# A kept row of squares, one filler fewer and swapped squares in a fused attention and MLP kernel

## The chip, the cores and the metric

The kernel runs on one core of one Trainium2 chip. The metric is the device time of one execution in microseconds (us). Every profile comes from one such execution; its span, from the first to the last instruction, is about 1.8 us shorter than the time of the same execution.

Names used below: PE is TensorE (matmuls), PEld its weight loads, DVE is VectorE, ACT is ScalarE, POOL is GpSimd and SP is SyncE (after the first microseconds both only issue transfers here). L217 is line 217 of the kernel. The changed kernel has one line more, so its lines from 493 on are numbered one higher: L578 before is L579 after.

## The reference, cut to what matters

```python
def _attn_ref(q, k, v, tau):                  # B, N, C = 4, 6080, 256
    qn = q / (np.linalg.norm(q, axis=1, keepdims=True) + 1e-06)
    kn = k / (np.linalg.norm(k, axis=1, keepdims=True) + 1e-06)
    s = kn.transpose(0, 2, 1) @ qn / tau
    ...                                       # softmax over the last axis -> a
    return (v @ a).astype(np.float32)

def _moe_ref(x, w_in, w_out, s, b):           # 24320 rows, 256 -> 2048 -> 256
    r = np.maximum(x @ w_in, 0.0)
    return ((s * (r * r) + b) @ w_out).astype(np.float32)
```

For each of four batches, the norms of q and k along N and the 256x256 product of k and q are needed before any row of that batch can go through the MLP. The kernel folds the softmax matrix into w_in (the result is called wa), so that the MLP runs straight from v.

## The kernel before

PE is the engine to keep fed. It runs 48 groups of up to 512 rows: a first product (h_ps, L578), relu on ACT, squares on DVE or ACT, and a second product (o_ps, L746) in a seven-product form that needs the sums S from DVE (in the first and the last group it is plain: L650, L624). While the groups of one batch run, the next batch's q and k are loaded in 12 chunks, and squares, products and norms are slipped in between by a table of steps.

The squares of one chunk are folded on DVE to one row tile `f` (128 partitions x 512). In batch 0 each row goes into the norm matmuls by itself. In batches 1 to 3 only the first row does: the rows of all later chunks are added into it by accumulating transfers.

```python
def fold(half, arrays, last):
    ...
        if last and (self.b == 0 or c == 0):
            self.rows.append((st["f", half], np_, 1))      # goes into the norm matmuls

def into_first():                                          # L188
    dst, src = self.rows[0][0][:np_], st["f", 1][:np_]
    po(nc.gpsimd.dma_start(out=dst, in_=src, accum_op=ALU.add))
...
ops += [fold(2, slice(0, 2), False), fold(1, slice(0, 2), True)]
return ops + [into_first] if self.b > 0 and c > 0 else ops

def add_norms(self, last=False):
    todo = [(t, np_, j, a, ch) for t, np_, jc in self.rows for j in range(jc)
            for a in range(2) for ch in range(CH)]         # 4 matmuls for each row
    for i, (t, np_, j, a, ch) in enumerate(todo):
        po(nc.tensor.matmul(self.n_ps[:, a, ch : ch + 1], t[:np_, a, j, ts(ch, P)],
                            ones16[:np_, 0:1], ...))       # L217, one column wide
```

At the start nothing else is there for PE. It runs matmuls that nobody reads ("fillers", L417) while DVE and ACT turn batch 0's norms and scores into wa:

```python
fin[1](); fin[2](); fin[3]()
keep_busy(5, w_in16[:, 0, :P], w_in16[:, 0, :NW])   # five 128x512 fillers
fin[4]()                                            # transposes of sm_s (L253)
...
```

In the last group every relu tile has its own square, alternating between DVE and ACT:

```python
if g in plain:
    late = g > 0 and m // 2 % 2 == 1
    square(g, m // 2, m // 2 + 1, nc.scalar if late else nc.vector)
```

Of the kernel before, what the change touches and what calls it, by code (L numbers as in the profile page):

```python
# [16 lines left out]
def kernel(  # L17
# [13 lines left out]
    P = 128  # L31
# [22 lines left out]
    def po(ins):  # L54

        tc.keep_in_program_order(ins)
        return ins
# [25 lines left out]
    w_in16 = wpool.tile([P, CH, Dff], FP16)  # L83
# [4 lines left out]
    def h_tile(name):  # L88
        return ps_h.tile([P, 2, TG], FP32, tag="h_ps", name=name)
# [19 lines left out]
    class Gram:  # L109
# [41 lines left out]
        def norm_ops(self, c):  # L151

            qc, kc = self.tiles[c]
            _, np_, jc = self.chunks[c]
            st = {}

            def squares(a, js):
                def f():
                    if "sq" not in st:
                        st["sq"] = sq_pool.tile([P, 2, JC, C], FP16, tag="sq", name="sq")  # L160
                    if a == 0:
                        po(nc.vector.tensor_mul(
                            st["sq"][:np_, 0, js, :], qc[:np_, js, :], qc[:np_, js, :]))
                    else:
                        po(nc.scalar.activation(  # L165
                            out=st["sq"][:np_, 1, js, :], in_=kc[:np_, js, :], func=AF.Square))
                return f

            def fold(half, arrays, last):
                def f():  # L170
                    src = st["f", 2 * half] if 2 * half < jc else st["sq"]
                    if ("f", half) not in st:
                        if last:
                            t = f3_pool.tile([P, 2, 1, C], FP16, tag="f3", name="f3")
                        else:
                            t = sq_pool.tile([P, 2, half, C], FP16, tag=f"f{half}", name="f")
                        st["f", half] = t
                    po(nc.vector.tensor_add(  # L178
                        st["f", half][:np_, arrays], src[:np_, arrays, :half, :],
                        src[:np_, arrays, half : 2 * half, :]))  # L180
                    if last and (self.b == 0 or c == 0):
                        self.rows.append((st["f", half], np_, 1))
                return f

# [5 lines that stand above are left out]
            def unfolded():  # L190
                self.rows.append((st["sq"], np_, jc))

            ops = []
            for h in range(0, jc, 4):
                js = slice(h, min(h + 4, jc))
                ops += [squares(1, js), squares(0, js)]
            if jc == 2:
                return ops + [unfolded]
            if jc == 8:
                ops += [fold(4, slice(0, 1), False), fold(4, slice(1, 2), False)]  # L200
            ops += [fold(2, slice(0, 2), False), fold(1, slice(0, 2), True)]
            return ops + [into_first] if self.b > 0 and c > 0 else ops

        def add_norms(self, last=False):

# [177 lines left out]
    NW = 512  # L383
# [29 lines left out]
    def keep_busy(n, w, x):  # L413

        idle_ps = h_tile("idle_ps")[:, 0, :]
        for _ in range(n):
            po(nc.tensor.matmul(idle_ps, w, x, start=True, stop=True, skip_group_check=True))  # L417

    for c in range(NCH0):
        ops = g0.norm_ops(c)  # L420
# [12 lines left out]
    fin[1]()  # L433
    fin[2]()
    fin[3]()
    keep_busy(5, w_in16[:, 0, :P], w_in16[:, 0, :NW])
    fin[4]()
    transpose_v(0)
    for f in fin[5:12]:
# [47 lines left out]
    def at_step(s, f):  # L487
        side.setdefault(int(s), []).append(f)


    FIN = (-12, 0, 3, 3, 6, 8, 10, 13)
    first_group = [b * N // TG for b in range(B)]
    for i, f in enumerate(fin[12:]):
        at_step(i // 2 * 4 - 1 + i % 2 if i > 1 else 0, f)
    at_step(14, lambda: po(nc.vector.tensor_scalar_mul(
        out=s_out, in0=s_bc, scalar1=1.0 / (LAM * LAM))))

# [63 lines left out]
    def mm1(g, m):  # L561

        _, nj = group(g)
        n = nj * P
        vT = vT_tiles[g]
        i, fh = divmod(m, 2)
        if fh == 0:
            h_tiles[g, i] = h_tile("h_ps")
        h_ps = h_tiles[g, i][:, fh, :]
        for b, p0, p1 in segments(g):  # L570
            wa = grams[b].wa
            for ci in range(CH):
                if p1 - p0 == P:
                    dst, src = h_ps[:, :n], vT[:, ci, :n]
                else:
                    dst = h_ps[:, :n].rearrange("f (j p) -> f j p", p=P)[:, :, p0:p1]
                    src = vT[:, ci, :n].rearrange("f (j p) -> f j p", p=P)[:, :, p0:p1]
                po(nc.tensor.matmul(dst, wa[:, ci, ts(m, P)], src,  # L578
                                    start=(ci == 0), stop=(ci == CH - 1), skip_group_check=True))  # L579
        if m == FT - 1:  # L580
            del vT_tiles[g]

    def relu(g, i):
        n = group(g)[1] * P
        if i % 2 == 0:
            r_tiles[g, i // 2] = rpool.tile([P, 2, 2, TG], FP16, tag="r16", name="r16")
        r16 = r_tiles[g, i // 2]
        po(nc.scalar.activation(out=r16[:, :, i % 2, :n], in_=h_tiles.pop((g, i))[:, :, :n],  # L588
                                func=AF.Relu))

    def square(g, i0, i1, engine):

        n = group(g)[1] * P
        if i0 == 0:
            g_tiles[g] = gpool.tile([P, 2, NP, TG], FP16, tag="g16", name="g16")
        src = r_tiles[g, i0 // 2][:, :, i0 % 2 : i0 % 2 + i1 - i0, :n]
        dst = g_tiles[g][:, :, i0:i1, :n]
        if engine is nc.scalar:
            po(nc.scalar.activation(out=dst, in_=src, func=AF.Square))  # L599
        else:  # L600
            po(nc.vector.tensor_mul(dst, src, src))  # L601
# [33 lines left out]
    def plain_mm2(g, m):  # L635

        _, nj = group(g)
        if g == NG - 1:
            last_mm2(0, m)
            if m == FT - 1:  # L640
                for i in range(FT):
                    last_mm2(1, i)
            return
        for h in range((nj + 1) // 2):
            js = [j for j in (2 * h, 2 * h + 1) if j < nj]
            if m == 0:
                o_plain[g, h] = ps_o.tile([P, 2, C], FP32, tag="o_ps", name="o_ps")
            o = o_plain[g, h]
            for j in js:
                po(nc.tensor.matmul(  # L650
                    o[:, j % 2, :], g_tiles[g][:, m % 2, m // 2, ts(j, P)],
                    w_out16[:, m, :], start=(m == 0 and j == js[0]),
                    stop=(m == FT - 1 and j == js[-1]), skip_group_check=True))
            if m == FT - 1:
                if h == 0:
                    o_sbs[g] = opool.tile([P, TG // P, C], FP32, tag="o_sb", name="o_sb")
                evacuate(o_sbs[g][:, js[0] : js[-1] + 1, :], o, rowconst, 1)
                if js[-1] == nj - 1:
                    store(g)
# [110 lines left out]
    for s in range(NS + FT):  # L770
        g, m = divmod(s, FT)
        if g < NG:
            mm1(g, m)

        if m == SHIFT and 0 < g and g - 1 not in plain:
            items = seven_items(g - 1)
            work.append((items, 8 if g == NG - 1 else 7))
        if work:
            items, n = work[0]
            for f in items[:n]:  # L780
                f()
            del items[:n]
            if not items:
                work.pop(0)
        for gp in plain:
            for mp in range(FT):
                if s == gp * FT + PLAG[gp] + (mp * 3 // 2 if gp == 0 else mp):
                    plain_mm2(gp, mp)
        if g < NG and m % 2 == 1:
            relu(g, m // 2)  # L790
            if g in plain:
                late = g > 0 and m // 2 % 2 == 1
                square(g, m // 2, m // 2 + 1, nc.scalar if late else nc.vector)
        if g < NG and g not in plain and m in SQUARES:
            square(g, *SQUARES[m])
        if g == NG - 1 and m in LAST:
            LAST[m]()
        elif m == 0 and 0 < g and g - 1 not in plain:
            square(g - 1, 6, 8, nc.vector)
        elif 0 < g and g - 1 not in plain and m in SUMS:  # L800
            sums_of(g - 1, SUMS[m])
        for f in side.pop(s, []):
            f()
# [34 lines left out]
```

## Time and profile before

| | before |
|---|---|
| time, median of 4 runs | 723.98 us (723.40 to 724.46; 723.81 of the three runs known at prediction time) |
| span of the profiled execution | 722.3 us |
| PE busy | 700.6 us (97%) |
| share of PE in the chain that ended last | 89% |
| largest wait of PE after 41 us | 1.4 us, for one accumulating transfer |

The lines that show the waits of PE stand in the prediction. A row of a timeline reads: start, duration, engine, line, operation, out<-in, shape, count, and in brackets the idle time before it with what ended it. Neighbouring instructions of one kind are merged into one row, and the end of a matmul is modelled; so I compare the starts of matmuls, which are not.

### The profile page before, as it was taken

What the parts mean: (1) busy time and instruction counts of PE and PEld (TensorE: products, weight loads), DVE (VectorE), ACT (ScalarE), POOL (GpSimd) and SP (SyncE); (2) the same over time, 40 slices, a digit from 0 to 9 for tenths busy, and PEclk for the clock granted to TensorE, in tenths of its full rate; (3) what the DMA queues carried; (4) which work ended last, traced back from release to release, by engine and by line L of the source; (5) the groups of instructions that cost most, each with busy time, mean ns of one, the idle gap of its engine ahead of it and who ended that gap; (6) DMA issues with size and microseconds to landing.
All of it is one profiled execution on the core that took longest, in us unless ns stands there. A gap on an engine that the chain in (4) does not pass through costs nothing.

```text
span 722.3 us, 17624 instructions
## 1 busy us (share of the span) xinstructions
PE 700.6 (97%) x7486; PEld 505.6 (70%) x7486; DVE 623.0 (86%) x871; ACT 544.8 (75%) x589; POOL 112.5 (16%) x191
## 2 busy tenths in 40 slices
PE   4799999999999999999999999999999999999997
PEld 2556777766677777777677777777668777777777
DVE  4779999988889999998788998998888888888886
ACT  5479877887777777788777777778777777777874
POOL 4522332111101222111010222111000000000000
PEclk9999999999999999999999999999999999999999
DMA  9999998556484979463763777836323333321202
GB/s 235 208 259 141 175 167 146 95 113 126 93 118 98 164 142 143 93 104 78 148 135 76 134 135 127 151 82 95 94 66 78 92 71 74 97 59 47 81 30 75
DMA packets 86447, 83.83 MB, mean 116 GB/s; under 512 B 56240, under 2 KB 61504, under 8 KB 86368
## 3 DMA queue, kind: packets, MB, share of 16 engines
q0 software_dynamic: 26176, 43.74, 37.6%
q1 hardware_dynamic: 59616, 37.64, 21.2%
q8 instruction: 59, 0.97, 0.6%
q10 hardware_dynamic: 576, 1.31, 0.5%
q14 instruction: 20, 0.16, 0.1%
HBM read 78.91 MB, written 24.90 MB: 144 GB/s over the span
## 4 chain that ended last, share of the span: by engine, by line
PE 89%; DMA 6%; issue 2%; DVE 1%; ACT 1%; POOL 1%; POOLq 0%; ACTq 0%
PE h_ps L578 43%; PE o_ps L746 38%; PE s_ps L142 4%; DMA qk<-in_q_dram 2%; PE wa_ps L290 2%; DMA f<-f 1%; DMA w_in<-in_moe_w_in_dram 1%; DMA qk<-in_k_dram 1%; ACT r L588 1%; POOL qk L126 1%; PE o_ps L624 1%; PE o_ps L650 0%; DVE S L672 0%; ACT g L599 0%; DVE o_sb L606 0%
## 5 line engine op out<-in xcount | busy, mean ns | idle before, releaser
L588 ACT ACTIVATE r<-h_ps 128x1024 f16<-128x1024 f32 (+1 forms) x384 | 388.0, 1014 | 144.3 <-PE h_ps L578 142.6
L578 PE MATMUL h_ps<-vT,wa 128*128 128x512 f16 (+7 forms) x1632 | 451.9, 364 | 0.6 <-ACT r L588 0.4
L746 PEld LDWEIGHTS <-S 128*128 128x128 f16 x2944 | 197.9, 98 | 85.2 <-DVE S L672 0.4
L746 PEld LDWEIGHTS <-g 128*128 128x128 f16 x2208 | 155.1, 98 | 74.0
L601 DVE TENSOR_TENSOR g<-r 128x2048 f16<-128x2048 f16 (+2 forms) x150 | 174.7, 1164 | 16.5 <-ACT r L588 16.2
L746 PE MATMUL o_ps<-T,S 128*128 128x128 f16 x2208 | 183.2, 219 | 0.3 <-DVE S L672 0.2
L578 PEld LDWEIGHTS <-wa 128*128 128x128 f16 x1632 | 136.2, 98 | 21.2 <-issue 1.0
L746 PE MATMUL o_ps<-w_out,g 128*128 128x128 f16 x1472 | 134.2, 219 | 0.3 <-DVE u L606 0.3
L606 DVE SCALAR_TENSOR_TENSOR o_sb<-o_ps,s_out,u 128x256 f32<-128x256 f32 x138 | 66.4, 481 | 50.1 <-PE o_ps L746 48.0
L599 ACT ACTIVATE g<-r 128x1024 f16<-128x1024 f16 (+1 forms) x97 | 100.4, 1035 | 0.2
L142 PE MATMUL s_ps<-qk 128*128 128x256 f16 (+1 forms) x384 | 69.4, 280 | 14.5 <-ACT qk L133 6.9
L337 POOL DMA_DIRECT2D v<-in_v_dram x48 | 31.9, 673 | 244.3 <-DMA vT<-v 179.8
L188 POOL DMA_DIRECT2D f<-f x33 | 28.9, 877 | 244.1 <-DVE f L178 186.4
L606 DVE SCALAR_TENSOR_TENSOR u<-o_ps,s_out,rowconst 128x256 f32<-128x256 f32 x138 | 65.9, 478 | 1.1 <-PE o_ps L746 1.1
L746 PE MATMUL o_ps<-w_out,S 128*128 128x128 f16 x736 | 63.5, 219 | 0.0
L746 PE MATMUL o_ps<-N,g 128*128 128x128 f16 x736 | 63.4, 219 | 0.0
L165 ACT ACTIVATE sq<-qk 128x1024 f16<-128x1024 f16 (+3 forms) x49 | 50.5, 1033 | 10.9 <-DMA qk<-in_k_dram 6.3
L674 DVE TENSOR_TENSOR S<-S,g 128x2048 f16<-128x2048 f16 (+1 forms) x47 | 56.4, 1201 | 1.3
L672 DVE TENSOR_TENSOR S<-g 128x2048 f16<-128x2048 f16 (+1 forms) x47 | 56.1, 1193 | 0.0
L678 DVE TENSOR_TENSOR S<-g,S 128x2048 f16<-128x2048 f16 x46 | 55.9, 1215 | 0.0
L676 DVE TENSOR_TENSOR S<-g 128x2048 f16<-128x2048 f16 x46 | 55.8, 1214 | 0.0
L142 PEld LDWEIGHTS <-qk 128*128 128x128 f16 (+1 forms) x384 | 32.5, 100 | 20.1 <-DVE qk L132 9.0
(72 smaller groups left out, 322.8 us busy)
## 6 DMA issues: line engine op xcount, KB each, us to landing
out_dram<-o_sb SPq DMA_DIRECT2D x46, 512.0 KB, 3.0
v<-in_v_dram POOLq DMA_DIRECT2D x47, 256.0 KB, 4.9
qk<-in_k_dram POOLq DMA_DIRECT2D x42, 256.0 KB, 6.1
qk<-in_q_dram POOLq DMA_DIRECT2D x42, 256.0 KB, 7.2
f<-f POOLq DMA_DIRECT2D x30, 128.0 KB, 3.1
vT<-v SPq DMA_TRANSPOSE x182, 3.2
w<-in_moe_w_out_dram POOLq DMA_DIRECT2D x4, 512.0 KB, 12.2
raw<-in_q_dram ACTq DMA_DIRECT2D x2, 512.0 KB, 6.4
```

Of the source, the lines that this page charges most:

```text
L142: po(nc.tensor.matmul(self.s_ps[:, ch, :], kc[:np_, j, ts(ch, P)], qc[:np_, j, :], start=(c == 0 and j == 0 and ch == 0), stop=(c == len(s ...
L165: po(nc.scalar.activation(out=st["sq"][:np_, 1, js, :], in_=kc[:np_, js, :], func=AF.Square))
L578: po(nc.tensor.matmul(dst, wa[:, ci, ts(m, P)], src, start=(ci == 0), stop=(ci == CH - 1), skip_group_check=True))
L588: po(nc.scalar.activation(out=r16[:, :, i % 2, :n], in_=h_tiles.pop((g, i))[:, :, :n], func=AF.Relu))
L599: po(nc.scalar.activation(out=dst, in_=src, func=AF.Square))
L601: po(nc.vector.tensor_mul(dst, src, src))
L606: po(nc.vector.scalar_tensor_tensor(out=dst, in0=src, scalar=s_out, op0=ALU.mult, in1=add, op1=ALU.add))
L672: po(nc.vector.tensor_add(T[1], A21, A22))
L674: po(nc.vector.tensor_sub(T[2], T[1], A11))
L676: po(nc.vector.tensor_sub(T[3], A11, A21))
L678: po(nc.vector.tensor_sub(T[4], A12, T[2]))
L746: po(nc.tensor.matmul(st[name][:, j, :], a()[:, i, ts(j, P)], w[:, i, :], start=first, stop=last, skip_group_check=True))
```

## The change

Its intent: the norms of batches 1 to 3 should not wait for the last accumulating transfer, so the last chunk's row stays a tile of its own and goes through four more norm matmuls. The opening gets one filler less. In the last group ACT and DVE swap squares, so that the very last square is on DVE, which is quicker at it (0.42 us against 0.63). A table named FOLDS replaces a formula.

```diff
-                    if last and (self.b == 0 or c == 0):
+                    if last and (self.b == 0 or c == 0 or c == len(self.chunks) - 1):
                         self.rows.append((st["f", half], np_, 1))
...
-            return ops + [into_first] if self.b > 0 and c > 0 else ops
+            return ops + [into_first] if self.b > 0 and 0 < c < len(self.chunks) - 1 else ops
...
-    keep_busy(5, w_in16[:, 0, :P], w_in16[:, 0, :NW])
+    keep_busy(4, w_in16[:, 0, :P], w_in16[:, 0, :NW])
...
+    FOLDS = (0, 0, 3, 4, 7, 8)
     for i, f in enumerate(fin[12:]):
-        at_step(i // 2 * 4 - 1 + i % 2 if i > 1 else 0, f)
+        at_step(FOLDS[i], f)
...
-                late = g > 0 and m // 2 % 2 == 1
+                late = g > 0 and m // 2 % 2 == 0
```

## The prediction

> **What bounds the kernel now.** I read the page first (busy shares, then the chain that ended last), then what TensorE (PE) waited for after the opening, then the timelines of the three places that the diff touches. All times are microseconds (us) of the profiled execution, which spans 722.3; the median of the timed runs is 723.81, and I carry a difference in span over to the time unchanged.
>
> ```profile
> PE 700.6 (97%) x7486; PEld 505.6 (70%) x7486; DVE 623.0 (86%) x871; ACT 544.8 (75%) x589; POOL 112.5 (16%) x191
> ...
> PE 89%; DMA 6%; issue 2%; DVE 1%; ACT 1%; POOL 1%; POOLq 0%; ACTq 0%
> ```
>
> PE is busy for 97% of the span and is 89% of the chain. So a change pays only where PE stands still, or where it removes PE work. The waits of PE from 40 us to the end are these:
>
> ```profile
> PE o_ps L217 <- DMA f<-f: 1.4, 1, 1.4
> PE h_ps L578 <- ACT r L588: 0.4, 1, 0.4
> PE o_ps L746 <- DVE u L606: 0.3, 1, 0.3
> PE wa_ps L290 <- DMA w_in<-in_moe_w_in_dram: 0.2, 1, 0.2
> PE o_ps L746 <- DVE S L672: 0.2, 1, 0.2
> ```
>
> Columns: total, times, longest. The largest is a single wait of the norm matmuls (L217) for the accumulating transfer that adds the last chunk's row of squares into the first row. It happens once, though there are three such batches. The chain and the timeline around it:
>
> ```profile
> 144.47 5.78 DMA f<-f
> ...
> 148.38 0.55 PE L746 MATMUL o_ps<-T,S 128*128 128x128 f16 x7
> ...
> 150.38 0.24 PE L217 MATMUL o_ps<-ones,f 128*128 128x1 f16 x4 [1.45 <-DMA f<-f]
> 150.48 0.59 PE L578 MATMUL h_ps<-vT,wa 128*128 128x512 f16 x2
> ```
>
> The transfer issued at 144.47 landed at 150.25, and PE started its four matmuls 0.13 later. In batch 2 the same place has no wait:
>
> ```profile
> 322.89 0.55 PE L746 MATMUL o_ps<-T,S 128*128 128x128 f16 x7
> 323.29 0.24 PE L217 MATMUL o_ps<-ones,f 128*128 128x1 f16 x4
> 323.39 0.59 PE L578 MATMUL h_ps<-vT,wa 128*128 128x512 f16 x2
> ```
>
> There the norms follow the seven matmuls after 0.40, start to start. In batch 3 they start at 496.20, also unhindered.
>
> **What the Trainium skill says.** "TensorE: Matmul & The Clock Gate", section "Wait — 56ns, not 53.3ns?", states that matmul starts never come closer than about 25 ns however narrow the matmul. The trace agrees: the 40 one-column norm matmuls of batch 0 take 1.14, the last of them 0.163 long, so (1.14 - 0.163)/39 = 0.025 each. Section "What's actually happening" there states that an idle window of about 3.4 us halves PE's clock; the mean granted clock of this run is 1.000, also in 35 to 40.1, where the filler goes. "DMA: Bandwidth & Descriptors", section "Anatomy of one DMA — SWDGE (gpsimd) path", fits a transfer as about 2.0 us plus bytes/436e3, an estimate of 2.3 for these 112 KB. The trace disagrees upward: the accumulating transfers land after 3.1 (median), batch 2's last after 3.0, batch 1's last after 5.8, because a store (144.60), four transposes (145.04) and a v load (145.09) were issued just behind it. "ScalarE: Activation LUTs", section "What ACT_TABLE_LOAD costs", gives 186 ns + 0.833 ns per element with immediate operands, 0.61 for 512; the trace has 0.63 for the 128x512 square on ScalarE (ACT), and 0.42 for the same square on VectorE (DVE).
>
> **The change part by part.**
>
> *Last row kept apart (batches 1 to 3).* It removes three transfers, one a batch, and adds one row to the norm matmuls: eight instead of four, as the order of the built kernel confirms. PE cost: 3 x 4 x 0.025 = +0.30. PE gain in batch 1: without the wait, L217 would start 0.40 after 148.38, as in batch 2, so at 148.78 instead of 150.38: -1.60 (the 1.45 shown as idle starts from a modelled matmul end). What the norms still need is there in time: the last row's fold on DVE ends at 143.76 + 0.42 = 144.18, and the next-to-last accumulation is issued at 138.06; with the usual 3 it lands near 141, and even at the 6.6 maximum of these transfers at 144.7, four us early. Does the gained 1.6 stay? DVE is the busiest neighbour (80.8 of the 84.3 us from 66 to 150.3), but it waits for PE just behind the norms, 1.05 at 151.52 and 1.46 at 157.60, so it can follow; ACT waits for PE in between too. Sum of the part: -1.60 + 0.30 = -1.3. Batches 2 and 3 by themselves lose 0.1 each.
>
> *One filler fewer.* A filler costs (1.25 - 0.38)/4 = 0.22 of PE. But what follows it waits elsewhere:
>
> ```profile
> 35.25 1.25 PE L417 MATMUL idle_ps<-w_in 128*128 128x512 f16 x5 [0.19 <-DMA w_in<-in_moe_w_in_dram]
> ...
> 36.42 0.53 PEld L253 LDWEIGHTS t_ps<-ident,sm_s 128*128 128x128 f32 x4 [0.41 <-issue]
> ...
> 40.13 1.04 PE L290 MATMUL wa_ps<-w_in,eT 128*128 128x512 f16 x4 [0.24 <-DMA w_in<-in_moe_w_in_dram]
> ```
>
> The transposes need the two sm_s scalings of DVE, which run from 35.82 to 36.69. The first pair could load some 0.1 sooner, but the second pair loads at 36.75, right behind the second scaling. And anything gained there ends at 40.13, where PE waits for the second piece of w_in; its 10.01 us in flight, issued at 30.07, owe nothing to the filler. Worth: 0.0.
>
> *The FOLDS table.* The old formula gives for the six folds 0, 0, 3, 4, 7, 8: the same numbers. The built order shows no move. Worth: exactly 0.
>
> *Squares of the last group swapped between ACT and DVE.* At the end:
>
> ```profile
> 715.05 0.60 ACT L588 ACTIVATE r<-h_ps 128x512 f16<-128x512 f32 x1 [0.96 <-PE h_ps L578]
> ...
> 715.68 0.63 ACT L599 ACTIVATE g<-r 128x512 f16<-128x512 f16 x1
> ...
> 716.36 0.11 PEld L624 LDWEIGHTS <-g 128*128 128x128 f16 x2 [0.30 <-ACT g L599]
> ```
>
> From 715.85 PE issues three matmuls of 0.11, so the fourth could start at 716.18 but waits for the last square until 716.36: 0.18 lost. On DVE the square would run from 715.68 to 716.10, and PE would go on at 716.18: -0.18. The swap also moves the second square (i=1) onto DVE ahead of an S sum and of a u evacuation, and the first onto ACT ahead of the second relu. By durations: relu 705.39 to 705.99, square to 706.65, next relu (0.1 overlap) to 707.15, DVE square 707.18 to 707.59, sum to 708.20, evacuation to 708.59 instead of 708.42. The product that overwrites that bank then starts near 708.65 instead of 708.48, +0.17; the next step, at 709.41 behind its own 0.15 wait for DVE, then needs none (second sum done at 709.19), so of the 0.17 about 0.02 remains. Sum of the part: -0.16.
>
> Total: -1.3 - 0.16 = about -1.45, so 723.81 becomes 722.36; I say 722.4.
>
> **The rivals.**
> *(a) Another transfer takes over the wait.* The first row is still written by the accumulation of chunk 10, and the v load behind it moves forward from 145.09 to about 139. For: one transfer of this kind did take 6.6. Against: it has 10.7 us, from 138.06 to 148.78. If so, the time stays at about 723.8 to 724.1.
> *(b) The wait is smaller without the profiler, or differs by run.* It hangs on the landing of one transfer among others; batch 2's landed in 3.0. At a 3 us landing nothing waits, and only the +0.3 and the tail are left: 723.9. The before runs, 723.4 to 724.46, are a us apart, so it may vary. I take a partial weight for this in the upper side of the range.
> *(c) The filler's removal counts fully:* another -0.2, 722.2. Against it stands the w_in wait. *Or it lets PE's clock drop:* 4 us of PE work at half speed could cost some us; the gap it opens is 0.2, far below the window named above.
> *(d) DVE becomes the bound of the tail:* if its new order holds PE up by more than reckoned, the part turns from -0.16 to about +0.2: 722.7.
>
> **Range and chances.** The mechanism of the one large term is read directly from the trace, so I expect a gain between 0.5 and 2.3: 721.5 to 723.3. A 2% change would be 14.5 us; no wait in the profile is that large, and nothing added is. Faster by over 2%: 0.01, within 2%: 0.98, slower by over 2%: 0.01.
>
> **What would show it.** Right: no wait of L217 for f<-f; L217 about 0.40 after the seven matmuls before it, with eight matmuls in 0.34; L290 still starting near 40.1 behind w_in; the last 18 output matmuls following the three before them without a gap; a span near 720.9. Wrong: a wait of L217 on the remaining accumulation or on DVE; a new wait of PE after 150 for DVE that gives the 1.6 back; L290 starting earlier than 40.0 by the filler; a longer wait of L746 for S near 708 to 709; a granted clock below 1 near 36.

## The result, and the profile after

The changed kernel took 722.88 us (median of 4 runs, 722.77 to 723.23) against 723.98 (4 runs): 1.1 us less. The ratio is 0.9986, with a 95% interval from 0.9969 to 1.0003. A ratio is the mean time of one kernel's runs over that of the other's of the same rounds, so not quite the ratio of the medians quoted. The interval includes 1: these eight runs alone do not separate the two kernels. A second set of the same pair does (after_again, below: 722.70 against 724.15, 0.9967 to 0.9994). The profiled execution spans 721.1 us instead of 722.3.

What PE waited for from 40 us to the end (total, times, longest), in the changed kernel:

```profile
PE wa_ps L290 <- DMA w_in<-in_moe_w_in_dram: 0.5, 1, 0.5
PE h_ps L579 <- ACT r L589: 0.4, 1, 0.4
PE o_ps L747 <- DVE u L607: 0.3, 1, 0.3
PE o_ps L747 <- DVE S L673: 0.2, 1, 0.2
```

The wait of L217 for f<-f is gone, no new row has come, and the wait for w_in has grown from 0.2 to 0.5. The timeline at batch 1's norms:

```profile
148.74 0.55 PE L747 MATMUL o_ps<-T,S 128*128 128x128 f16 x7
149.13 0.34 PE L217 MATMUL o_ps<-ones,f 128*128 128x1 f16 x8
149.34 0.59 PE L579 MATMUL h_ps<-vT,wa 128*128 128x512 f16 x2
```

The eight norm matmuls start 0.39 after the seven matmuls before them, where before it was 2.00, and the first product follows 0.21 later instead of 0.10. The opening:

```profile
35.62 1.04 PE L417 MATMUL idle_ps<-w_in 128*128 128x512 f16 x4 [0.38 <-DMA w_in<-in_moe_w_in_dram]
...
36.56 0.53 PEld L253 LDWEIGHTS t_ps<-ident,sm_s 128*128 128x128 f32 x4 [0.40 <-issue]
...
40.50 0.82 PE L290 MATMUL wa_ps<-w_in,eT 128*128 128x512 f16 x3 [0.47 <-DMA w_in<-in_moe_w_in_dram]
```

Four fillers instead of five, and yet the wa matmuls start at 40.50 instead of 40.13: the second piece of w_in came later (in flight 10.40 us instead of 10.01). The end, in the chain that ended last:

```profile
714.55 0.45 PE o_ps L747 x8
715.00 2.31 PE o_ps L625 x21
717.30 0.03 issue
717.33 0.48 DVE o_sb L631
```

All 21 last output matmuls run as one piece. In the kernel before they were 3 and 18 with a pause between them.

To see where the 1.2 us of span went, I read four points from the profiles: T1, start of the 512-wide wa matmuls (L290), which wait for w_in; T2, batch 1's norms; T3, batch 3's norms; T4, the start of the last evacuation (the scaled copy of a finished product to its output tile) on DVE, from which all of them need 3.75 to 3.79 to the end. Spans between them, in us, for the kernels that differ only by parts of the change (the experiments below explain the names):

| kernel | T1 | T1 to T2 | T2 to T3 | T3 to T4 | T4 |
|---|---|---|---|---|---|
| before | 40.13 | 110.25 | 345.82 | 222.34 | 718.54 |
| after | 40.50 | 108.63 | 346.00 | 222.20 | 717.33 |
| rows_only | 40.45 | 108.64 | 346.00 | 222.42 | 717.51 |
| swap_only | 40.21 | 109.87 | 345.82 | 222.11 | 718.01 |
| filler_only | 40.11 | 109.99 | 345.82 | 222.33 | 718.25 |
| rows_b1 | 40.23 | 108.65 | 345.92 | 222.33 | 717.13 |
| best | 40.39 | 108.64 | 345.92 | 222.11 | 717.06 |
| after_again | 40.22 | 108.64 | 345.99 | 222.20 | 717.05 |

From before to after: +0.37 up to T1, -1.62 to T2, +0.18 to T3, -0.14 to T4, together -1.21.

### The profile page after: what moved, and what is told of

Its sections match the earlier page's. It is cut to its first block, busy times and chain, and to the rows that moved or that the text cites. A ratio compares the mean times of both kernels' runs of the same rounds, so it can differ in the third digit from the quotient of the medians.

```text
span 721.1 us, 17642 instructions
## 1 busy us (share of the span) xinstructions
PE 700.9 (97%) x7497; PEld 506.3 (70%) x7497; DVE 622.5 (86%) x871; ACT 544.7 (76%) x589; POOL 109.1 (15%) x188
## 4 chain that ended last, share of the span: by engine, by line
PE 91%; DMA 5%; ACT 1%; DVE 1%; POOL 1%; issue 0%; ACTq 0%; POOLq 0%
PE h_ps L579 44%; PE o_ps L747 40%; PE s_ps L142 4%; DMA qk<-in_q_dram 2%; PE wa_ps L290 2%; DMA w_in<-in_moe_w_in_dram 1%; DMA qk<-in_k_dram 1%; ACT r L589 1%; POOL qk L126 1%; PE o_ps L625 0%; PE o_ps L651 0%; ACT g L600 0%; PE t_ps L253 0%; DVE o_sb L607 0%; DVE sq L162 0%
## 5 line engine op out<-in xcount | busy, mean ns | idle before, releaser
L188 POOL DMA_DIRECT2D f<-f x30 | 26.3, 876 | 225.1 <-DVE f L178 194.7
```

## The experiments

The theory and its rivals are those of the prediction. Every experiment but after_again edits the kernel before. Kernels are compared only within the same rounds. All gave correct results.

### Each part alone

**rows_only** has the first two hunks of the diff above, **swap_only** the last one, **filler_only** `keep_busy(4, ...)`.

> The kernel before with the kept row alone. My theory: the wait of the batch-1 norm matmuls goes (-1.60 us start to start), twelve more one-column matmuls come (+0.30 us), so -1.3 us: about 722.7 against 724.0 for the kernel before, span near 721.0, no wait of L217 for f<-f. Rival (the wait is smaller in unprofiled runs): the timed difference is clearly under 1 us while the profiled span shows 1.3. Rival (another transfer takes over): L217 still waits for f<-f.

> The kernel before with the swapped squares of the last group alone. My theory: the 0.18 us pause before the last 18 output matmuls goes and the pause of 0.15 us near 709 shrinks a little, so the stretch from the batch-3 norms (496.2 in the kernel before) to the end shortens by 0.15 to 0.25 us; the timed difference is below what the timing resolves. The wait of L217 stays at about 1.4 us. Rival (DVE holds PE up in its new order): the stretch is equal or longer.

> The kernel before with four instead of five fillers. My theory: 0.0 us; the second pair of transposes still follows the second sm_s scaling, and the matmuls of the 512-wide wa pieces still wait for w_in; their start moves only with the landing of w_in. Rival (the filler is on the path): 0.2 us less. Rival (the clock drops): granted clock below 1 around 36 us and longer.

Five runs each, against 724.20 us for the kernel before (9 runs): rows_only 723.05 us (ratio 0.9986, interval 0.9974 to 0.9999), swap_only 723.91 us (0.9995, 0.9983 to 1.0008), filler_only 724.01 us (0.9999, 0.9986 to 1.0011). So the kept row is nearly the whole of it, also over the runs whose traces were not kept. Every run lists a span and a granted clock; whether the wait is smaller without the profiler is therefore not tested. The table is sharper than the timing: the kept row alone gives -1.61 up to T2 and +0.18 +0.08 after it; the swap alone gives -0.23 after T3; the filler alone leaves T1 where it was, at 40.11.

The wait itself is not one number. With the old transfers T1 to T2 was 110.25, 109.87 and 109.99 in three profiles, and without the wait 108.63 to 108.65 in all five: the wait was worth 1.6, 1.2 and 1.35. That half confirms the rival "differs by run"; the one profile that I predicted from was at the upper end.

### The kept row in batch 1 alone

```diff
-                    if last and (self.b == 0 or c == 0):
+                    if last and (self.b == 0 or c == 0
+                                 or (self.b == 1 and c == len(self.chunks) - 1)):
...
-            return ops + [into_first] if self.b > 0 and c > 0 else ops
+            return ops + [into_first] if (self.b > 0 and c > 0 and not
+                                          (self.b == 1 and c == len(self.chunks) - 1)) else ops
```

> The row kept apart in batch 1 alone; batches 2 and 3 accumulate as before. My theory: it keeps the whole gain of 1.60 us and pays only one of the three surcharges of 0.10 us, so -1.5 us against the kernel before and 0.2 us better than the kept row in all batches. Rival (the transfers that stay in batches 2 and 3 do cost something there): no better than the kept row everywhere.

722.79 us against 724.20 (ratio 0.9981, interval 0.9968 to 0.9995), 0.26 us below rows_only; the runs of the two overlap a little (722.58 to 723.08 and 723.01 to 723.63). The profile shows the two saved surcharges: 345.92 instead of 346.00 between T2 and T3, and 222.33 instead of 222.42 after T3. The rival, that the transfers of batches 2 and 3 cost something, is not borne out: their norms start 0.39 and 0.40 after the matmuls before them with the transfer kept.

### The accumulating transfer later, and earlier

```diff
  (acc_late: only the last fold and the transfer of the last chunk)
-                    at_step(int(sc) + 2 + 1 + i * 3, f)
+                    at_step(int(sc) + 2 + 1 + i * 3
+                            + (3 if i > 2 and c == len(gr.chunks) - 1 else 0), f)
  (acc_early: all of the last chunk's steps closer together)
-                    at_step(int(sc) + 2 + 1 + i * 3, f)
+                    at_step(int(sc) + 2 + 1 + i * (3 if c < len(gr.chunks) - 1 else 2), f)
```

> The kernel before with the last fold of the last chunk three steps later on DVE (about 2.5 us), and so its accumulating transfer too. My theory: in batch 1 every us of lateness goes into the wait of L217, so it grows from 1.4 to between 3 and 4 us and the time by 2 to 2.5 us (or less if the transfer, behind the store and the transposes, lands faster than in 5.8); batches 2 and 3 have some 4 us of slack and show no wait. Rival (the wait is only an inference of the profile and PE was held by something else): the time does not move.

acc_late took 728.06 us against 724.27 (ratio 1.0055, interval 1.0040 to 1.0070, 4 runs): 3.8 us more, where I expected 2 to 2.5. Start to start beyond the usual 0.39, the norms of the profiled run waited 2.13, 0.92 and 1.94 us in the three batches, 5.0 together instead of 1.6. In batch 1 the wait grew by only 0.5, because the later transfer landed in 3.2 us instead of 5.8. Batches 2 and 3, which should not have waited, did. There the transfers were issued 4.2 us before the norms could start, instead of 6.9: 2.7 us later, as meant. The 3.0 us that they take in the kernel before would have been soon enough, but from the chain:

```profile
321.78 5.02 DMA f<-f
...
495.58 6.05 DMA f<-f
```

In their new place a store (0.13 us later), a transpose (0.57) and a v load (0.63) were issued right behind them, the company that the slow transfer of batch 1 has in the kernel before. Besides, in the profiled run the clock fell. The norms of batch 1, and then stretches of 1 us (columns: stretch, length, busy time of PE, PEld, DVE, ACT and POOL with counts, granted clock, DMA share, GB/s):

```profile
151.46 0.24 PE L217 MATMUL o_ps<-ones,f 128*128 128x1 f16 x4 [1.97 <-DMA f<-f]
```

```profile
152.00:153.00 1.00, 1.00 (x11) 0.67 (x10) 0.40 (x2) 0.75 (x1) 0.00 (x0) 0.85 1.04 170
153.00:154.00 1.00, 1.00 (x9) 0.80 (x8) 1.00 (x2) 0.28 (x1) 0.00 (x0) 0.50 0.41 71
...
156.00:157.00 1.00, 1.00 (x11) 0.66 (x10) 0.62 (x2) 1.00 (x1) 0.00 (x0) 0.94 0.64 41
```

About 1.2 us after the pause of 1.97, PE's clock went to 0.50, and it stayed there for 0.30 + 3 + 0.12 = 3.4 us. The way from batch 1's norms to batch 2's, less batch 2's wait, took 174.56 us instead of 172.91: 1.65 lost. That run spans 727.8; the other three span 725.4 to 726.3 at a mean clock of 1.000, which fits the longer waits alone (722.3 + 3.4); their traces were not kept. In batch 3 of the profiled run a pause of 1.77 left the clock at 1.00. That PE really is held by this transfer is settled all the same: the rival said that the time would not move.

> The kernel before with the folds of the last chunk two steps apart instead of three, so that its accumulating transfer can start about 2 to 3 us sooner, with no extra matmuls. My theory: issued near 142 it is ahead of the store (144.6) and the transposes (145.0), lands in about 3 us, and the wait of L217 goes: -1.6 us against the kernel before, 0.3 better than the kept row. Rival (DVE, busy 97% there, delays an S sum or a u evacuation): new waits of PE for DVE of some tenths between 139 and 146, which take part of it back.

acc_early took 723.38 us against 724.27 (ratio 0.9988, interval 0.9972 to 1.0005): -0.9 instead of -1.6. The transfer was issued at 142.43, landed in 3.0 us, and the wait went. But my rival came true as well. PE and DVE near 140:

```profile
140.25 0.33 PE L746 MATMUL o_ps<-T,S 128*128 128x128 f16 x3
140.73 0.38 PE L746 MATMUL o_ps<-w_out,S 128*128 128x128 f16 x4
```

```profile
138.46 1.22 DVE L678 TENSOR_TENSOR S<-g,S 128x2048 f16<-128x2048 f16 x1
139.59 0.69 DVE L178 TENSOR_TENSOR f<-sq 112x1024 f16<-112x1024 f16 x1
140.19 0.48 DVE L606 SCALAR_TENSOR_TENSOR o_sb<-o_ps,s_out,u 128x256 f32<-128x256 f32 x1
```

Three 128-wide matmuls (0.17 of issue) are followed only after 0.48. The square now stands before the S sum on DVE and the first fold before the evacuation: the sum ran from 138.46, in rows_b1 from 137.79. This pause of 0.31 and a second one of 0.05 at 142.59 come in batch 1, and T2 to T3 is 346.15 instead of 345.82, 0.33 more in batches 2 and 3 (in batch 2 the three matmuls at 313.62 are followed after 0.28 instead of 0.17). Here, moving work earlier on the busiest neighbour costs more than four narrow matmuls.

### What slows that one transfer

One v load, issued by the same queue right behind the late transfer (145.09), is moved ahead of it:

```diff
-            at_step(max(g - 4, 0) * FT + 2, lambda g=g: load_v(g))
+            at_step(max(g - 4, 0) * FT + 2 - (18 if g == 12 else 0), lambda g=g: load_v(g))
```

> The kernel before with one v load (the one issued right behind the late accumulation) moved ahead of it. It asks what made that transfer take 5.8 instead of 3 us. If the v load of the same queue delays it: landing in about 3 to 4 us and hardly a wait. If the store and the transposes of the other queue do (my guess, since the v load was issued after it): still about 5 to 6 us and the same wait of about 1.4.

723.42 us against 724.27 (ratio 0.9988, interval 0.9973 to 1.0003). Transfer issues of POOL, and PE at the norms:

```profile
139.22 1.36 POOL L337 DMA_DIRECT2D v<-in_v_dram  x2
144.99 0.89 POOL L188 DMA_DIRECT2D f<-f  x1 [4.41 <-DVE f L178]
```

```profile
148.90 0.55 PE L746 MATMUL o_ps<-T,S 128*128 128x128 f16 x7
149.91 0.24 PE L217 MATMUL o_ps<-ones,f 128*128 128x1 f16 x4 [0.45 <-DMA f<-f]
```

The transfer landed after 4.8 us and the wait was 0.62 (1.01 less 0.39). My guess of "the same wait of about 1.4" was wrong, and so was the other answer of "hardly a wait". With the v load behind it, the five profiles of this transfer at its old place show 5.1, 5.4, 5.5, 5.7 and 5.8 us. In acc_early, issued 2 us before the store (144.6 in the kernel before) and the transposes (145.0), it landed in 3.0 although two v loads followed it at 143.07; in acc_late, issued at 148.10, it landed in 3.2. All accumulating transfers of the 13 profiles say the same. The 47 that had both a store and a transpose issued within 1.3 us behind them took 4.2 to 6.6 us, the 40 of them without a v load in the first us as well; the 98 with neither a store nor a transpose in flight took 2.7 to 3.0; the 273 between these, with part of that company, took anything from 2.7 to 6.6. So the slow landing comes with the store and the transposes, and the v load is not needed for it. Which of the two does it, and whether the v load adds anything, is left open: 4.8 is one sample, inside that range. Nor is it the only way to be slow: in batch 3 of acc_early a transfer took 4.7 us with only two v loads behind it for the first 4.4.

### Fillers

```diff
-    keep_busy(5, w_in16[:, 0, :P], w_in16[:, 0, :NW])
+    keep_busy(0, ...)      (fill0)
+    keep_busy(8, ...)      (fill8)
```

> The kernel before with no filler at that place. My theory: 0.0 us, w_in still ends the wait near 40.1 to 40.5. Rival (fillers on the path, 0.22 us each): 1.1 us less. Rival (the clock needs them): granted clock below 1 between 36 and 40, matmuls of 0.43 instead of 0.22 us, and a longer time.

fill0 took 724.54 us against 724.27 (ratio 1.001, interval 0.9995 to 1.0026; runs 724.30, 724.31, 724.77 and 726.73). The profiled run is the 726.73 one. PE at the transposes, and stretches of 1 us around it:

```profile
36.76 1.08 PE L253 MATMUL t_ps<-ident,sm_s 128*128 128x128 f32 x4 [1.39 <-DVE sm_s L242]
```

```profile
36.00:37.00 1.00, 0.24 (x1) 0.27 (x2) 0.89 (x3) 0.99 (x2) 0.50 (x2) 0.72 1.05 208
37.00:38.00 1.00, 1.00 (x8) 0.89 (x8) 0.01 (x1) 0.22 (x2) 0.43 (x1) 0.50 1.13 224
...
43.00:44.00 1.00, 1.00 (x6) 0.37 (x4) 0.52 (x1) 0.44 (x2) 0.42 (x1) 0.86 1.00 340
```

Without fillers PE pauses 1.39 us for DVE, and the clock was 0.50 for 0.56 + 6 + 0.28 = 6.8 us. The 512-wide wa matmuls started at 41.57 instead of 40.13, and no longer behind w_in. Another of the four runs has a mean clock of 0.996, the other two of 1.000 and 0.999: the fall came in some runs only. So the rival "the clock needs them" holds for all five fillers, but not for the one that the change takes away: filler_only and both sets of the changed kernel show mean clocks of 0.999 or 1.000 in all 14 runs. One to three fillers were not tried.

> Eight fillers instead of five. My theory: they end 0.65 us later, the transposes and what follows shift by about 0.5 us, which is just what PE otherwise spends waiting for w_in: its 512-wide wa matmuls start at most 0.2 us after w_in has landed, so the span moves by no more than that. Rival (fillers count fully): 0.65 us longer.

One look at 723.47 us (state unknown, as for any single run). The fillers end later, and PE goes on without a pause:

```profile
39.78 0.59 PE L578 MATMUL h_ps<-vT,wa 128*128 128x512 f16 x2
40.23 1.04 PE L290 MATMUL wa_ps<-w_in,eT 128*128 128x512 f16 x4
```

The wa matmuls start 0.45 after two 512-wide ones, which take 0.43 to issue, and 0.05 after w_in landed (40.18), the same lag as in every profile that waits for it. So PE now arrives level with w_in. T1 is 40.23, within the 40.11 to 40.69 that it has in the others but fill0, with w_in landing anywhere from 40.06 to 40.64. The slack that w_in leaves is about three fillers. The shorter span (721.7) is not the fillers' doing: the batch-1 wait happened to be 0.91 here.

### A version that combines the better choices

**best** is rows_b1 with the swap, and five fillers. **after_again** is the changed kernel once more.

> Row kept apart in batch 1 alone, squares of the last group swapped, five fillers as before. My theory adds the parts as measured in the traces: -1.6 + 0.1 for the row, -0.23 for the swap, so about -1.7 us against the kernel before and 0.2 us below the changed kernel (it saves two surcharges of 0.10). Rival (the parts overlap, or the difference drowns in the landing of w_in, which differed by 0.5 us among the runs so far): no better than the changed kernel.

> The changed kernel once more, on the same chip and rounds as the one before it in this call. About -1.3 to -1.6 us against the kernel before, granted clock 0.999 or 1.000 in every run (four fillers were enough in all runs so far, none was not).

best took 722.51 us (722.35 to 722.96), after_again 722.70 us (722.62 to 722.84), the kernel before 724.15 us (9 runs); ratios 0.9979 (0.9966 to 0.9991) and 0.9980 (0.9967 to 0.9994). The runs of the two overlap, so the timing does not separate them. The profiles do: from T1 to T4 best needs 676.67 us and after_again 676.83. The difference of 0.16 is the two surcharges saved. Against the kernel before, -1.64 was measured where -1.7 was expected, and -1.45 where -1.3 to -1.6 was.

## Why the prediction was right or wrong

*The wait of batch 1 (predicted -1.60, from the profile of one run).* Right in mechanism and, between the two profiles compared, in size: -1.62. Rival (a), another transfer takes over, did not happen: the accumulation of chunk 10 was issued at 138.42 and landed at 141.13, eight us before it was needed, although two v loads now followed it at once. Rival (b) was partly right: 0.91 to 1.61 in five profiles. The timed gain of the kept row alone, 1.15 us between medians, is near what -1.2 to -1.6 and the surcharge below make.

*The reason for the slow landing.* The prediction states it as a fact that the transfer took 5.8 us because a store, transposes and a v load came just behind it. That was a guess when it was written. The runs bear out the company of the store and the transposes (4.2 to 6.6 us against 2.7 to 3.0); a part of the v load in it is not shown.

*The surcharge (predicted +0.30).* Measured +0.18 and +0.08, so +0.26. Each four extra one-column matmuls take 0.10 or a little less, as reckoned from the spacing of 25 ns.

*The gain stays.* Right: T2 to T3 and T3 to T4 are equal to a few hundredths in all kernels but for the surcharges and the swap. DVE followed, as its own waits for PE had promised.

*The filler (predicted 0.0).* Right: filler_only has T1 at 40.11, and fill8 shows that even three more would not have counted. The later T1 of the changed kernel's first profile (40.50) is the landing of w_in, which went from 40.06 to 40.64 over the profiles where it is waited for, with four and with five fillers alike; after_again had 40.22. This is what kept the first pair of profiles at -1.21 instead of -1.58. The fear for the clock was unfounded for one filler and well founded for five.

*The table.* Right by the order of instructions alone; nothing there moved.

*The swap (predicted -0.16).* Measured -0.23 in swap_only and -0.24 in the changed kernel (222.34 to 222.20, with +0.10 for the last surcharge in it). The pause of 0.18 before the last matmuls went as predicted. The step near 709 also went as told: the pause moved one step ahead. In the chain of the changed kernel:

```profile
706.88 0.45 PE o_ps L747 x8
707.65 0.58 PE o_ps L747 x8
708.56 0.45 PE o_ps L747 x8
```

Eight matmuls take 0.45 without a pause. The 0.13 extra is now in the second of these steps; in the kernel before it was 0.16, one step later. So the mis-sized term is the remainder of the second square: I reckoned +0.02 and it was -0.03. The last few hundredths are not traced.

*The sum.* -1.45 predicted; -1.10 and, in the second set, -1.45 measured between medians; -1.21 and -1.5 between the spans. That the second set meets -1.45 to the hundredth is luck: the wait alone varied from 0.91 to 1.61. The time of 722.88 lies in the stated range of 721.5 to 723.3.

## What to carry to other kernels

When the bounding engine is 97% busy, list its few waits, and take the gain of a removed wait from starts of instructions, not from idle times with modelled ends. Apply a cure only where its wait is: the kept row paid in one batch of three. A wait for a transfer among others is a spread and not a number, so look at several runs before putting two decimals on it. And taking something off an engine that then waits for a transfer anyway wins nothing, while taking all of it away can cost the clock.

## What the Trainium skill lacked or had wrong

- "TensorE: Matmul & The Clock Gate", section "What's actually happening", ties the halved clock to at least one idle window of about 3.4 us. Here it fell to 0.50 after PE pauses of 1.97 us (acc_late) and 1.39 us (fill0, amid sparse work, in the profiled run), but not after the 1.45 us of the kernel before, nor after 1.77 us in batch 3 of acc_late. The lengths of the slow stretches, 3.4 and 6.8 us, do agree with one and two such windows. The page gives no share of a window that must be busy, which is what one would need to know.
- "DMA: Bandwidth & Descriptors", section "Anatomy of one DMA — SWDGE (gpsimd) path", has a fit that gives an estimate of 2.3 us for the 112 KB transfer. Accumulating transfers landed in 2.7 to 3.0 us with no store or transpose in flight, and in 4.2 to 6.6 us with a store and a transpose issued within 1.3 us behind them.
- No page consulted has a time for an accumulating SBUF-to-SBUF transfer; the runs give 2.7 to 3.0 us for 112 to 128 KB with no store or transpose in flight.
